# A new order table for an attention and feed-forward kernel: the step-2 load of w moves ahead of the first weights

## The chip, the cores and the metric

The kernel runs on 1 core of one Trainium2 chip. The metric is device time in microseconds (us) of one execution, the median of several runs. A core has five engines that run side by side and meet by semaphores: TensorE (PE, with its weight loads as PEld), VectorE (DVE), ScalarE (ACT), GpSimd (POOL) and SyncE (SP), which here issues all DMA transfers.

## The reference

Two stages, in float32. The first is a recurrent attention with 4 batches, 8 heads, 768 tokens and head size 48. The second is a feed-forward layer on the 3072 tokens with 384 features, whose weights go from 384 to 2048 and back.

```python
for t in range(S):                       # per batch b and head h
    y[t] = r[t] @ (state + outer(u * k[t], v[t]))
    state = w[t][:, None] * state + outer(k[t], v[t])
x = y as (3072, 384)
out = relu(x @ w_in) ** 2 @ w_out
```

## The kernel before

The tokens of a batch are cut into 3 steps of 256, so there are 12 steps, numbered 0 to 11; each works on all 8 heads. A step is a chain of some 40 short operations:

- **Loads** (`ld`, SP): w, r, k and v of a step come in four transfers of 384 KB each (line 212). u is one small row (line 240). The four groups of the first weights, `ld.0.i` to `ld.3.i` (line 220), and the four of the second, `ld.0.o` to `ld.3.o` (line 225), have 768 KB each. Each is cast to 16 bits by `cast` (line 232) on an engine that the order names.
- **Decay**: `ww_` multiplies neighbouring w (line 297), `lw_` takes the logarithm on ACT (301), `cum_` makes running sums by matmuls (341 to 345), `exp_` the exponential on ACT (358), `ni_` helps it on DVE in late steps (353), `ac_` the factors for the state (363). `rw_` and `kw_` are products of r and k with w (309, 313). `rd_` makes the decayed r and k on DVE (376).
- **Transposes of them**: steps 0 to 2 by matmuls (`tr_`, 385) and a copy (`rkt_`, 390). Steps 3 to 11 use two DMA transposes that SP issues (`dtr_`, 393).
- **Scores**: `p_` (410), then the mask product `pm_` on DVE (418 or 421).
- **Bonus term**: `ku_`, `qp_`, `q_`, `vq_` (316, 321, 324, 327).
- **State**: `su_` (433), `ts_` (441, 443), `sn_` (447).
- **Output of attention**: `y_`, `yq_`, `yc_`, `yb_`, `yd_` (460), copied by `ysb_` (510, 512). It is transposed by matmuls and a copy in steps 0 to 3 (`yt_` 520, `xt_` 525), by a DMA from step 4 on (`dyt_`, 528).
- **First layer**: `m1_`, 8 groups of 6 matmuls in a step, called expansion groups here (538). A group needs the cast weights of one of the four groups and one of four PSUM banks. `rl_` empties the bank with a relu (545 on ACT, 547 on DVE), `sq_` squares (553, 555).
- **Second layer**: steps 0 to 4 by `m2_`, 8 groups of 4 matmuls (561), emptied by `os_` (567, 569). Steps 5 to 11 use a scheme with 7 block products instead of 8: `tw_` and `sw_` make sums (580, 593), `pw_` are the products (615), `cx_` and `ow_` combine them (620 to 634).
- **Stores** (`store`, SP, 639), and **warm-up** matmuls without a result (`warm_`, 643).

No scheduler decides the order. It is written out as a string of 934 words, `ORDER`, and one loop turns each word into its instructions in turn. Each engine runs its own instructions strictly in that order, so an instruction that waits holds up all that stands behind it on its engine. A word can end with the engine (`=A` ACT, `=V` DVE, `=G` POOL) and can name its PSUM bank (`:2`).

```python
for word in ORDER.split():
    word, _, engine = word.partition("=")
    word, _, bank = word.partition(":")
    name, *args = word.split(".")
    args = tuple(int(x) if x.isdigit() else x for x in args)
    where[(name,) + args] = engine
    ...
    operations[name](*args)
```

So `rl_.5.3=A` is the relu of group 3 of step 5 on ScalarE. Buffers are handed out by a small helper in the same order: w, r, k and v have four buffers each, so that a load can run up to four steps ahead of its use.

Of the kernel before, what the change touches and what calls it, by code (L numbers as in the profile page):

```python
# [22 lines left out]
cast.i.0=A ld.2.r rkt_.1.1=V tr_.1.0:2 y_.0 rkt_.1.0=V yq_.0 ts_.0.1=V p_.1.1:n ku_.1=G ysb_.0.1=A p_.1.0:1 sn_.0.1=G
pm_.1.1 ysb_.0.0=A yt_.0.1:2 cast.i.2=A su_.1:0 yt_.0.0:3 xt_.0.1=V xt_.0.0=V qp_.1=V m1_.0.0:2 ts_.1.0=V cast.i.1=A
q_.1 sn_.1.0=G pm_.1.0 m1_.0.4:0 m1_.0.1:3 m1_.0.5:1 rl_.0.0=A m1_.0.2:2 vq_.1=G cast.i.3=A y_.1:1 rl_.0.1=V rl_.0.5=V
yc_.1 yq_.1 rl_.0.4=V yd_.1 ww_.2=V ld.0.o m1_.0.3:1 ld.2.v ysb_.1=A ts_.1.1=V m1_.0.7:3 ld.1.o lw_.2 rl_.0.3=V
sn_.1.1=G rl_.0.2=A yt_.1:0 kw_.2=G cum_.2:0 xt_.1=V m1_.0.6:1 rl_.0.7=V exp_.2 ld.4.w ld.3.w ld.2.o rd_.2.1 m1_.1.0:2
rw_.2=G rl_.0.6=A ld.3.o ku_.2=G rl_.1.0=A m1_.1.2:3 m1_.1.4:1 sq_.0.0=A rd_.2.0 tr_.2.1:0 m1_.1.6:2 rl_.1.2=V
rl_.1.4=A m1_.1.1:1 rl_.1.6=V qp_.2=G m1_.1.7:3 rkt_.2.1=V tr_.2.0:2 rl_.1.7=V v_.2=G m1_.1.3:0 rkt_.2.0=V cast.o.0=A
m1_.1.5:3 ac_.2 cast.o.1=G ld.3.k sq_.0.2=A sq_.0.1=A rl_.1.1=V m2_.0.1.0:2 rl_.1.3=A q_.2 sq_.1.0=A p_.2.1:0 su_.2:1  # L30
vq_.2=G sq_.1.1=A m2_.0.1.1 m2_.0.0.0:0 m2_.1.0.0:1 ts_.2.0=V ld.3.r sn_.2.0=G pm_.2.1 m2_.1.0.1 ww_.3=G yc_.2:1
sq_.0.3=A rl_.1.5=A cast.o.2=A yq_.2 p_.2.0:0 sq_.1.2=V m2_.0.0.1 m2_.1.1.0:3 pm_.2.0 lw_.3 sq_.1.3=A m2_.0.0.2
ww_.4=G cum_.3:0 ld.3.v ld.4.r ld.4.k exp_.3 kw_.3=G cast.o.3=A yb_.2 y_.2 m2_.1.1.1 ku_.3=V m2_.1.1.2 m2_.0.1.2
rd_.3.1 rw_.3=G ysb_.2=A lw_.4 m2_.0.1.3 m2_.1.1.3 dtr_.3.1 qp_.3=G rd_.3.0 cum_.4:1 ac_.3 exp_.4 os_.0.1=A os_.1.1=V
m2_.1.0.2 yt_.2:3 tw_.3=V m2_.0.0.3 xt_.2=A rw_.4=G q_.3 m2_.1.0.3 dtr_.3.0 os_.0.0=A kw_.4=G ku_.4=G m1_.2.2:3 ac_.4
os_.1.0=A rd_.4.0 m1_.2.0:0 rl_.2.2=A m1_.2.3:2 ld.4.v v_.3=A rd_.4.1 m1_.2.1:3 rl_.2.0=A su_.3:1 ld.5.w rl_.2.3=A
ld.5.k ld.5.r vq_.3=V p_.3.0:0 rl_.2.1=A ld.7.w m1_.2.6:1 m1_.2.4:2 ts_.3.0=V pm_.3.0 sq_.2.0=A sn_.3.0=G m1_.2.7:3
v_.4=G rl_.2.6=A ts_.3.1=V tw_.1=V yc_.3:1 yq_.3 sq_.2.1=A rl_.2.4=A rl_.2.7=A p_.3.1:0 m2_.2.1.0:0 m1_.2.5:1 ld.5.v
pm_.3.1 rl_.2.5=V ww_.5=G lw_.5 sq_.2.3=A qp_.4=V q_.4 sn_.3.1=G rw_.5=G kw_.5=G y_.3 store.0.1 yb_.3 su_.4:0 dtr_.4.0
m2_.2.0.0:2 ts_.4.0=V ww_.7=G ysb_.3=A m2_.2.0.1 sq_.2.2=A yt_.3:3 cum_.5:1 m2_.2.1.1 m2_.2.0.2 m2_.2.1.2 exp_.5  # L40
sn_.4.0=V store.1.1 rd_.5.1 dtr_.4.1 xt_.3=A m2_.2.1.3 ts_.4.1=V rd_.5.0 v_.5=G vq_.4=G ld.6.w os_.2.1=A m1_.3.4:1
m1_.3.2:3 m1_.3.0:0 ld.6.k rl_.3.4=A ac_.5 rl_.3.2=A rl_.3.0=A dtr_.5.1 sn_.4.1=V ku_.5=V qp_.5=V tw_.2=V m2_.2.0.3
su_.5:1 p_.4.1:0 m1_.3.5:3 ts_.5.0=V os_.2.0=A rl_.3.5=A m1_.3.1:0 pm_.4.1 m1_.3.3:2 dtr_.5.0 rl_.3.1=A m1_.3.7:3
sq_.3.0=A kw_.6=G rl_.3.3=V yc_.4:1 yq_.4 p_.4.0:0 m2_.3.1.0:1 pm_.4.0 sq_.3.2=A sq_.3.1=A rl_.3.7=A m1_.3.6:2 ld.6.r
ld.7.k ld.8.k ww_.6=G sn_.5.0=G ku_.6=G y_.4 yb_.4 ysb_.4=A q_.5 p_.5.0:0 pm_.5.0 store.2.1 m2_.3.1.1 m2_.3.0.0:0
vq_.5=G lw_.6 dyt_.4 tw_.4=V cum_.6:1 p_.5.1:0 rw_.6=G pm_.5.1 rl_.3.6=A exp_.6 m2_.3.0.1 m2_.3.0.2 m2_.3.1.2 ld.7.r
rd_.6.1 ku_.7=G lw_.7 sq_.3.3=A ld.6.v yc_.5:0 yq_.5 y_.5 m2_.3.1.3 dtr_.6.1 os_.3.1=A qp_.6=V rd_.6.0 kw_.7=G
# [653 lines left out]
```

## Time and profile before

| | |
|---|---|
| median of 3 runs | 178.3 us (177.92 to 178.44) |
| the profiled execution's own time | 178.94 us |
| its span, first to last instruction | 177.2 us |
| PE busy | 167.7 us (95%) |
| DVE busy | 148.6 us (84%) |
| ACT busy | 128.6 us (73%) |
| POOL busy | 113.1 us (64%) |
| DMA moved | 36.58 MB, mean 206 GB/s |
| granted TensorE clock, mean | 1.000 |

Busy time is the time in which an engine has an instruction under way. A row of the timeline reads: start in us from the span's start, duration in us, engine, line of the kernel, operation, out<-in, shapes, and in brackets the idle time of the engine just before it with what ended it. SPq is the queue in which SyncE issues transfers; its durations are those of the issue, not of the transfer. Matmuls are pipelined, so a row's duration for a group is a little longer than the distance to the next group.

### The profile page before, as it was taken

The page shows a single profiled execution, that of the slowest core. Times are in us where ns is not written, and L with a number is a line of the kernel's source. Part 1 is how long each engine was busy: PE and PEld are TensorE (multiplying, and loading weights), DVE is VectorE, ACT ScalarE, POOL GpSimd, SP SyncE. Part 2 cuts the span into 40 slices and gives each one's busy share as a digit, 9 for nine tenths or more (in the row PEclk, how much of TensorE's full clock was granted, in tenths as well). Part 3 has the DMA queues.
Part 4 walks back from the last instruction along what each step waited for, and adds up shares of the span by engine and source line. Part 5 has one row for each costly group of instructions (what it writes and reads, how often), then busy time and mean ns, then how long its engine had stood idle before and what let it go on. Part 6 is the DMA issues. An engine that isn't in the chain of part 4 may idle for free.

```text
span 177.2 us, 6475 instructions
## 1 busy us (share of the span) xinstructions
PE 167.7 (95%) x2772; PEld 132.9 (75%) x2774; DVE 148.6 (84%) x235; ACT 128.6 (73%) x213; POOL 113.1 (64%) x108
## 2 busy tenths in 40 slices
PE   7877899999999999999999999999999999999992
PEld 2344778756687686578866888878998988999991
DVE  5588998965999798989979998999989899559671
ACT  5574888989799579739697896888887584867200
POOL 6399359794974929997459367683547690572910
PEclk9999999999999999999999999999999999999999
DMA  5999999999998999998999999998697211420204
GB/s 151 315 311 350 367 266 357 230 369 286 218 257 233 237 256 191 304 253 101 286 199 306 233 156 286 172 238 236 134 257 67 51 45 41 140 89 4 89 10 167
DMA packets 82669, 36.58 MB, mean 206 GB/s; under 512 B 75857, under 2 KB 81106, under 8 KB 82642
## 3 DMA queue, kind: packets, MB, share of 16 engines
q1 hardware_dynamic: 82642, 36.19, 83.3%
q8 instruction: 21, 0.34, 0.8%
q14 instruction: 6, 0.05, 0.1%
HBM read 25.17 MB, written 4.72 MB: 169 GB/s over the span
## 4 chain that ended last, share of the span: by engine, by line
PE 76%; DMA 13%; POOL 4%; DVE 2%; SPq 1%; issue 1%; ACT 0%; DVEq 0%
PE one L538 29%; PE one L615 18%; PE one L561 15%; PE att L460 6%; DMA rkT_b<-rdec_buf 6%; DMA w_st_b<-in_moe_w_out_dram 5%; PE att L410 3%; DMA u_row<-in_u_dram 2%; PE att L433 2%; SPq L212 1%; POOL ku_b L316 1%; PE att L343 1%; POOL wo_sb L232 1%; DVE pmT_b L418 1%; POOL k_b L313 1%
## 5 line engine op out<-in xcount | busy, mean ns | idle before, releaser
L538 PE MATMUL one<-xT_b,wi_sb 128*128 128x256 bf16 x576 | 70.9, 273 | 0.5 <-DVE xT_b L525 0.5
L538 PEld LDWEIGHTS <-wi_sb 128*128 128x128 f16 x576 | 54.7, 98 | 9.1 <-issue 1.2
L545 ACT ACTIVATE gt_b<-one 128x512 f16<-128x512 f32 x73 | 42.1, 598 | 16.2 <-PE one L538 14.8
L553 ACT ACTIVATE gt_b<-gt_b 128x1024 bf16<-128x1024 f16 x39 | 40.1, 1052 | 0.1
L561 PE MATMUL one<-wo_sb,gt_b 128*128 128x384 f16 x160 | 29.5, 326 | 0.4 <-POOL wo_sb L232 0.4
L421 DVE TENSOR_TENSOR pmT_b<-att,mask 128x1024 bf16<-128x1024 f32 x22 | 26.8, 1218 | 1.9 <-PE att L410 1.8
L615 PEld LDWEIGHTS <-gt_b 128*128 128x128 bf16 x280 | 23.5, 98 | 0.6 <-issue 0.2
L561 PEld LDWEIGHTS <-gt_b 128*128 128x128 bf16 x160 | 14.8, 98 | 9.5 <-issue 0.6
L547 DVE TENSOR_SCALAR gt_b<-one 128x512 f16<-128x512 f32 x23 | 15.5, 684 | 3.2 <-ACT gt_b L545 1.9
L447 POOL TENSOR_TENSOR S_b<-t_b,ac_buf 128x192 bf16<-128x192 f32 x16 | 8.8, 551 | 13.8 <-DVE t_b L443 7.7
L327 POOL TENSOR_TENSOR vq_b<-v_b,q_b 128x768 bf16<-128x768 f32 x10 | 15.5, 1550 | 2.7 <-DVE q_b L324 2.7
L615 PE MATMUL one<-wo_sb,gt_b 128*128 128x192 f16 x168 | 16.5, 246 | 0.0
L316 POOL TENSOR_TENSOR ku_b<-k_b,u_bc 128x768 f32<-128x768 f32 x8 | 14.5, 1815 | 2.9 <-ACT u_bc L249 1.8
L313 POOL TENSOR_TENSOR k_b<-k_b,w_b 128x384 f32<-128x384 f32 x10 | 11.0, 1099 | 7.1 <-DMA k_b<-in_k_dram 7.1
L321 POOL TENSOR_TENSOR ku_b<-ku_b,r_b 128x768 f32<-128x768 f32 x8 | 14.9, 1858 | 0.5 <-DVE pmT_b L421 0.4
L309 POOL TENSOR_TENSOR r_b<-r_b,w_b 128x384 f32<-128x384 f32 x9 | 10.7, 1185 | 5.0 <-DMA r_b<-in_r_dram 4.8
L324 DVE TENSOR_REDUCE q_b<-ku_b 128x16 f32<-128x768 f32 x12 | 11.4, 946 | 1.7 <-POOL ku_b L321 1.7
L376 DVE TENSOR_TENSOR rdec_buf<-k_b,att 128x768 bf16<-128x768 f32 (+1 forms) x13 | 11.4, 885 | 1.0 <-POOL k_b L313 0.9
L376 DVE TENSOR_TENSOR rdec_buf<-r_b,att 128x768 bf16<-128x768 f32 (+1 forms) x13 | 11.5, 885 | 0.3 <-POOL r_b L309 0.3
L358 ACT ACTIVATE att<-att 128x768 f32<-128x768 f32 x12 | 9.6, 797 | 2.7 <-PE att L345 2.3
L615 PE MATMUL one<-w_st_b,gt_b 128*128 128x192 f16 x112 | 11.4, 246 | 0.0
L593 POOL TENSOR_TENSOR w_st_b<-w_st_b,gt_b 128x512 bf16<-128x512 bf16 x4 | 5.0, 1250 | 7.5 <-DVE w_st_b L593 7.5
(105 smaller groups left out, 281.8 us busy)
## 6 DMA issues: line engine op xcount, KB each, us to landing
w_b<-in_w_dram SPq DMA_DIRECT2D x12, 384.0 KB, 5.0
r_b<-in_r_dram SPq DMA_DIRECT2D x12, 384.0 KB, 5.0
k_b<-in_k_dram SPq DMA_DIRECT2D x12, 384.0 KB, 5.2
v_b<-in_v_dram SPq DMA_DIRECT2D x12, 384.0 KB, 4.5
out_dram<-w_st_b SPq DMA_DIRECT2D x23, 192.0 KB, 2.7
w_st_b<-in_moe_w_in_dram SPq DMA_DIRECT2D x4, 768.0 KB, 7.9
w_st_b<-in_moe_w_out_dram SPq DMA_DIRECT2D x4, 768.0 KB, 7.7
rkT_b<-rdec_buf SPq DMA_TRANSPOSE x18, 4.4
```

Of the source, the lines that this page charges most:

```text
L313: product("kw_", s)(k_raw[:, :, 0, :], k_raw[:, :, 1, :], w_raw[:, :, 1, :])
L316: product("ku_", s)(buf("ku", s)[:], buf("k", s)[:, :, 1:3, :], u_bc[:, :, None, :].to_broadcast([C, H, 2, D]))
L321: product("qp_", s)(ku[:], ku[:], buf("r", s)[:, :, 0:2, :])
L327: product("vq_", s)(buf("vq", s)[:].rearrange("p j h d -> p h j d"), buf("v", s)[:], buf("q", s)[:, :, :, None].to_broadcast([C, H, 2, D]))
L376: nc.vector.tensor_mul(rdec[:, i, :, heads, 0:D], x.rearrange("p h j d -> p j h d"), decay[:, None, :, :].to_broadcast([C, 2, n, D]))
L421: nc.vector.tensor_mul(pmT, ps_p[:].rearrange("p e (a x) -> p (e a) x", a=2), mk.to_broadcast([C, 4, 2 * C]))
L538: nc.tensor.matmul(ps1[:, j, :], wi_sb[:, n // 4, kk, n % 4 * 128:(n % 4 + 1) * 128], xT[:, :, kk, :], start=(kk == 0), stop=(kk == KT - 1))
L545: nc.scalar.activation(rl, m1, AF.Relu, scale=RS)
L547: nc.vector.tensor_scalar(out=rl, in0=m1, scalar1=RS, scalar2=0.0, op0=ALU.mult, op1=ALU.max)
L553: nc.scalar.activation(gt, rl, AF.Square)
L561: nc.tensor.matmul(m2, gt[:, n, c * C:(c + 1) * C], wo_sb[:, n, :], start=(n == 0), stop=(n == NT - 1))
L615: nc.tensor.matmul(where_to, gt[:, n, :], wo[:, n, :], start=(n == 0 and i in (1, 2, 5)), stop=(n == NT // 2 - 1), skip_group_check=True)
```

## The change

The string `ORDER` is replaced as a whole; all functions stay as they are. The new string has the same 934 words of work in another sequence, with other banks and, for some, another engine. Counted over the words: `qp_` 3 more on POOL and 3 fewer on DVE, `vq_` 2 more on POOL and 2 fewer on DVE, `rw_` 3 more on DVE and 3 fewer on POOL, `v_` 2 on DVE and 1 on ACT taken from POOL, `sq_` and `sw_` 3 each off DVE (to ACT and to POOL), `cast` 2 off ACT (one to POOL, one to DVE), `rl_` and `os_` 2 each from ACT to DVE. The warm-up matmuls are 28 instead of 24. One pair of lines of the diff stands for the rest:

```diff
-ld.0.w ld.0.r warm_.2.3 ld.0.k ld.0.u ww_.0=V lw_.0 ld.0.v warm_.9.0 rw_.0=G ld.1.w ld.1.r cum_.0:1 kw_.0=V exp_.0
+ld.0.w ld.0.k ww_.0=V warm_.7.2 ld.0.r warm_.3.1 ld.0.u ld.1.w lw_.0 ld.0.v cum_.0:0 ld.1.r exp_.0 warm_.4.2 rw_.0=V
```

First place: SyncE at the start of the program, the loads of steps 0 and 1 and the first of step 2. The buffers w_b_68, 69 and 70 hold w of steps 0, 1 and 2; the next transfers are the four groups of the first weights.

```order
 L212 DMA w_b_68<-in_w_dram 128x8x96
+L212 DMA k_b_76<-in_k_dram 128x8x96
 L212 DMA r_b_72<-in_r_dram 128x8x96
-L212 DMA k_b_76<-in_k_dram 128x8x96
 L240 DMA u_row<-in_u_dram 1x384
+L212 DMA w_b_69<-in_w_dram 128x8x96
 L212 DMA v_b_80<-in_v_dram 128x8x96
-L212 DMA w_b_69<-in_w_dram 128x8x96
 L212 DMA r_b_73<-in_r_dram 128x8x96
 L212 DMA k_b_77<-in_k_dram 128x8x96
+L212 DMA w_b_70<-in_w_dram 128x8x96
 L212 DMA v_b_81<-in_v_dram 128x8x96
```

k and r of step 0 change places (both stand ahead of u in either order), w of step 1 goes ahead of v of step 0, and w of step 2 is now ahead of v of step 1 and of the weights; before, it was issued behind all four weight groups.

Second place: ScalarE around the casts of the first weights (the w_st buffers), the y_sb copies of step 0 (y_sb_b_112, in two halves) and step 1 (y_sb_b_113), and the first evacuations (gt_b). First the rows of before:

```order
L305 CAST v_bf_b_91<-v_b_81 128x768
L232 CAST wi_sb<-w_st_b_84 128x1536
L512 CAST y_sb_b_112<-att_62 128x384 x2
L232 CAST wi_sb<-w_st_b_85 128x1536
L232 CAST wi_sb<-w_st_b_86 128x1536
L545 ACTIVATE gt_b_118<-one_66 128x512
L232 CAST wi_sb<-w_st_b_87 128x1536
L510 CAST y_sb_b_113<-att_63 128x768
```

And the rows of the changed kernel:

```order
L305 CAST v_bf_b_91<-v_b_81 128x768
L390 COPY rkT_b_101<-one_65 128x1024
L232 CAST wi_sb<-w_st_b_84 128x1536
L512 CAST y_sb_b_112<-att_62 128x384 x2
L232 CAST wi_sb<-w_st_b_85 128x1536
L232 CAST wi_sb<-w_st_b_86 128x1536
L232 CAST wi_sb<-w_st_b_87 128x1536
L545 ACTIVATE gt_b_118<-one_66 128x512
L301 ACTIVATE lw_buf_134<-ww_b_88 128x8x48
L510 CAST y_sb_b_113<-att_63 128x768
```

The evacuation that stood between the third and fourth cast moves behind the fourth, and the logarithm of step 2 goes ahead of the copy of step 1. The groups come in the order 0, 2, 1, 3 before and 1, 0, 2, 3 now; the expansion groups of step 0 are reordered to match (0, 4, 1, 5, 2, 3, 7, 6 before; 2, 0, 1, 5, 4, 7, 3, 6 now).

Third place: SyncE at the DMA transposes of steps 4 (rkT_b_100) and 5 (rkT_b_101), with stores of steps 0 to 2 (out_dram) and loads. First the rows of before:

```order
L639 DMA out_dram<-w_st_b_84 128x384
L393 DMA_TRANSPOSE rkT_b_100<-rdec_buf_140 128x8x128
L639 DMA out_dram<-w_st_b_84 128x384
L393 DMA_TRANSPOSE rkT_b_100<-rdec_buf_140 128x8x128
L212 DMA w_b_68<-in_w_dram 128x8x96
L212 DMA k_b_78<-in_k_dram 128x8x96
L393 DMA_TRANSPOSE rkT_b_101<-rdec_buf_141 128x8x128 x2
```

And the rows of the changed kernel:

```order
L639 DMA out_dram<-w_st_b_84 128x384
L393 DMA_TRANSPOSE rkT_b_100<-rdec_buf_140 128x8x128 x2
L393 DMA_TRANSPOSE rkT_b_101<-rdec_buf_141 128x8x128
L639 DMA out_dram<-w_st_b_84 128x384 x2
L393 DMA_TRANSPOSE rkT_b_101<-rdec_buf_141 128x8x128
L212 DMA w_b_71<-in_w_dram 128x8x96
```

The two transposes of step 5 stood next to each other behind two loads; now two stores stand between them. On TensorE the work between the running sums of step 5 and its first score matmuls becomes 3 output groups, 7 expansion groups and some small matmuls.

More of the change, by code (lines that the diff above doesn't have):

```diff
@@ L23 @@
[L23 to L47, printed above, removed]
@@ new lines @@
+yc_.0:0 tr_.1.1:0 yd_.0 yq_.0 rkt_.1.1=V y_.0 ts_.0.1=V p_.1.1:m sn_.0.1=G qp_.1=G cast.i.1=A pm_.1.1 ysb_.0.0=A
+ysb_.0.1=A p_.1.0:1 ld.3.w cast.i.0=A ld.2.v cast.i.2=A yt_.0.0:1 yt_.0.1:0 ww_.2=G su_.1:0 ld.2.r xt_.0.1=V xt_.0.0=V
+ts_.1.0=V q_.1 m1_.0.2:1 m1_.0.0:3 m1_.0.1:0 rl_.0.0=V pm_.1.0 vq_.1=G sn_.1.0=G m1_.0.5:2 ld.0.o m1_.0.4:3 rl_.0.1=V
+rl_.0.2=V cast.i.3=A ts_.1.1=V kw_.2=G rl_.0.5=A lw_.2 y_.1:1 yq_.1 yc_.1 ld.1.o yd_.1 m1_.0.7:2 ysb_.1=A ku_.2=V
+cum_.2:0 ld.3.r ld.3.k ww_.3=G rl_.0.7=A yt_.1:1 exp_.2 m1_.0.3:0 xt_.1=V m1_.0.6:2 rl_.0.3=A m1_.1.0:1 rd_.2.1
@@ L94 @@
+store.11.1.0
 """
```

119 lines of the change are left out of this document (69 added, 50 removed).

## The prediction, on record before the result

> **What bounds the kernel now.** I read the page first, then the busy time by stretch, then the timeline of the first 37 us and the chain that ended last. From the page: busy time of the engines, and two lines of the span in 40 slices of 4.43 us.
>
> ```profile
> PE 167.7 (95%) x2772; PEld 132.9 (75%) x2774; DVE 148.6 (84%) x235; ACT 128.6 (73%) x213; POOL 113.1 (64%) x108
> PE   7877899999999999999999999999999999999992
> DMA  5999999999998999998999999998697211420204
> ```
>
> TensorE is the bound: 167.7 of 177.2 us, with full slices from the fifth one on. The DMA line is full from the second slice to the twenty-eighth, so in the first 20 us transfers are what everything else runs after. The busy time by stretch (columns: stretch, length, then PE, PEld, DVE, ACT and POOL busy, clock, DMA share, GB/s) shows where TensorE still waits:
>
> ```profile
> 10.00:15.00 5.00, 3.38 (x66) 1.82 (x67) 4.62 (x7) 2.86 (x7) 5.00 (x6) 1.00 1.05 325
> 15.00:20.00 5.00, 3.98 (x147) 3.02 (x144) 4.11 (x9) 3.50 (x4) 3.84 (x4) 1.00 1.01 355
> ...
> 70.00:80.00 10.00, 9.87 (x174) 6.37 (x169) 8.52 (x10) 5.73 (x12) 9.64 (x8) 1.00 1.16 282
> ...
> 100.00:110.00 10.00, 9.60 (x196) 8.23 (x194) 9.35 (x15) 7.57 (x13) 5.26 (x5) 1.00 1.09 200
> 110.00:120.00 10.00, 9.59 (x231) 8.18 (x225) 9.11 (x15) 9.02 (x16) 7.76 (x8) 1.00 1.08 216
> ```
>
> From 40 to 170 us all other stretches are full, so the idle time there is 0.13 + 0.40 + 0.41 = 0.94 us. A matmul's modelled end overlaps the next one by about 0.2 us, so each wait is really that much longer than its idle time; five of them make about 2.0 us. That is all that a new order can win behind 40 us. Both orders hold the same TensorE work, but for four more warm-up matmuls. So the time is: the start of the dense stream, plus the same work, plus the waits in it. The timeline of before, around that start:
>
> ```profile
> 16.50 1.47 ACT L232 CAST wi_sb<-w_st_b 128x1536 f16<-128x1536 f32 x1 [2.37 <-DMA w_st_b<-in_moe_w_in_dram]
> ...
> 17.88 0.85 ACT L512 CAST y_sb_b<-att 128x384 bf16<-128x384 f32 x2
> ...
> 20.00 2.23 PE L538 MATMUL one<-xT_b,wi_sb 128*128 128x256 bf16 x19 [0.50 <-DVE xT_b L525]
> ...
> 20.77 1.47 ACT L232 CAST wi_sb<-w_st_b 128x1536 f16<-128x1536 f32 x1 [0.66 <-DMA w_st_b<-in_moe_w_in_dram]
> ```
>
> ScalarE idles 2.37 us for the first weight group, which lands at about 16.5; the third holds it up again, at 20.7. The first expansion matmul starts at 20.00, 1.27 us behind the end of the two y_sb copies (18.73).
>
> **The change, part by part.** *Loads.* A load of one step's input is 393 kB; at the 325 GB/s of the row 10 to 15 that is 1.21 us. The changed order puts w of step 2 ahead of the four weight groups, with the queues full (share 1.05), so I move every weight landing by +1.2: the first from 16.5 to 17.7, the third from 20.7 to 21.9. The bounds are 0 (a queue with room) and 1.3. The last cast of before shows no DMA wait and starts when the one ahead of it has long ended:
>
> ```profile
> 22.86 1.47 ACT L232 CAST wi_sb<-w_st_b 128x1536 f16<-128x1536 f32 x1
> ...
> 26.77 2.78 PE L538 MATMUL one<-xT_b,wi_sb 128*128 128x256 bf16 x24
> ```
>
> ScalarE idles from 22.74 to 22.86 there, so I take 22.8 as the landing of the fourth group, and 24.0 after the change. The swap of k and r of step 0 costs nothing: each is ahead of u before and after, and the two products change engines with them.
>
> *The chain to the first expansion matmul.* On ScalarE the cast of the first weights stands ahead of the y_sb copies of step 0, before as after. Before, it ended at 17.97 and the copies hardly waited. Now it runs from 17.7 to 19.2, the copies to 20.05, and with the same 1.27 us behind them the first expansion matmul starts at 21.3: **+1.3**. The cover for this delay is gone, since what stands ahead of it on TensorE is the same as before. The second mask of step 0 goes later as well; on VectorE five operations now stand between the two masks. The first fence has groups of the whole span (count, busy us, mean ns), the second rows of the timeline:
>
> ```profile
> L327 POOL TENSOR_TENSOR vq_b<-v_b,q_b 128x768 bf16<-128x768 f32 x10 | 15.5, 1550 | 2.7 <-DVE q_b L324 2.7
> L321 POOL TENSOR_TENSOR ku_b<-ku_b,r_b 128x768 f32<-128x768 f32 x8 | 14.9, 1858 | 0.5 <-DVE pmT_b L421 0.4
> ...
> L321 DVE TENSOR_TENSOR ku_b<-ku_b,r_b 128x768 f32<-128x768 f32 x4 | 4.4, 1096 | 0.0
> ...
> L309 DVE TENSOR_TENSOR r_b<-r_b,w_b 128x384 f32<-128x384 f32 x3 | 1.8, 590 | 0.0
> ```
> ```profile
> 10.04 1.22 DVE L421 TENSOR_TENSOR pmT_b<-att,mask 128x1024 bf16<-128x1024 f32 x1
> ...
> 12.81 0.95 DVE L324 TENSOR_REDUCE q_b<-ku_b 128x16 f32<-128x768 f32 x1 [0.36 <-POOL ku_b L321]
> ...
> 14.73 0.95 DVE L376 TENSOR_TENSOR rdec_buf<-r_b,att 128x768 bf16<-128x768 f32 x1
> ...
> 18.13 1.29 DVE L418 TENSOR_TENSOR pmT_b<-one,mask 128x512 bf16<-128x512 f32 x2 [0.24 <-PE one L410]
> ```
>
> From the first mask's end (11.26): 0.59 + 1.10 + 0.95 + 2 x 0.95 + 1.29 = 5.83, so 17.1 at the earliest (some waits between make it 17.5), and the step's output matmuls end at 18.0. That hides behind the cast, which ends at 19.2; it costs 0.6 only if the weights land as early as before. The four more warm-up matmuls (0.24 each, priced below) fall into the wait between the sums of step 1 at 12 and its transposes at 15: 0. The other changes of engine go together: 3 products at 1.86 and 2 at 1.55 come to POOL, smaller ones leave it, so it rises from 64% by some 3%, and DVE falls as much. None comes near TensorE's 95%, so they cost 0 in sum and act only through the waits below.
>
> *From there to 36 us.* All four casts now stand ahead of the first evacuation on ScalarE. The fourth runs from 24.0 to 25.5; behind it come an evacuation (0.59), a logarithm (0.53) and the y_sb copy of step 1 (0.80), to 27.4, and only then can its transposes run on TensorE, with the last two expansion groups of step 0 behind them in order. Transposes (0.35) and two groups (0.66 each) from 27.5 put the first group of step 1 at 29.1. Before, that group was the second in the row at 26.77, at 27.43: **+1.7**. Part comes back where before waited for the second output weights:
>
> ```profile
> 33.87 1.47 POOL L232 CAST wo_sb<-w_st_b 128x1536 f16<-128x1536 f32 x1 [1.23 <-DMA w_st_b<-in_moe_w_out_dram]
> ...
> 34.55 0.41 PE L433 MATMUL att<-v_bf_b,rdec_buf 64*64 64x48 bf16 x16
> ...
> 35.38 1.78 PE L561 MATMUL one<-wo_sb,gt_b 128*128 128x384 f16 x10 [0.42 <-POOL wo_sb L232]
> ```
>
> The 16 state matmuls issue in 0.19 us, so TensorE lost 0.65 there, of which I return 0.3 (o1 lands at nearly the same time, but its cast is now on ScalarE behind a square of 1.05). That leaves **+1.4** at 36 us.
>
> *Behind 36 us.* Three places have less cover and two more. (1) In step 2 exp of step 3 stands ahead of the y_sb copy, 0.80 each, and only two output groups (0.65 each) stand between the output matmuls and the transposes: 0.4, bounds 0 to 0.8. (2) The transposes by DMA of step 5:
>
> ```profile
> 58.52 0.32 PE L345 MATMUL att<-lw_buf,tri_incl_neg 128*128 128x384 bf16 x1
> ...
> 60.92 0.95 DVE L376 TENSOR_TENSOR rdec_buf<-r_b,att 128x768 bf16<-128x768 f32 x1
> ...
> 62.82 3.95 SPq L393 DMA_TRANSPOSE rkT_b<-rdec_buf  x2
> ...
> 70.30 0.42 PE L410 MATMUL att<-rkT_b 64*64 64x128 bf16 x16
> ```
> ```profile
> 65.52 4.74 DMA rkT_b<-rdec_buf
> ```
>
> Before, 11.5 us pass from the end of the sums (58.84) to the score matmuls (70.30), and they wait about 0.2. After, TensorE holds 8.8 us of work there: 7 expansion groups x 0.66, 3 output groups x 0.65, and 2.2 of small matmuls. The chain needs exp (0.80), two decays (0.95 each), the first transpose's issue (1.3), two stores (1.1 each), then 4.74 with the last transpose: 10.9 at worst; with the stores issued early, 8.7. I take a wait of 0.8 instead of 0.2, so +0.6 (0 to 1.9). (3) At step 11 the copy (0.8) and the transpose stand against 7 groups of 0.66 = 4.6; before, 10 groups covered it.
>
> ```profile
> xT_b<-y_sb_b SPq DMA_TRANSPOSE x8, 3.8
> ```
>
> 0.8 + 3.8 + 0.2 makes +0.2 (0 to 0.7). In return, the idle 0.81 of the rows 100 to 120 can go. One of its two waits is this one, in the chain and the timeline:
>
> ```profile
> 109.79 5.81 DMA rkT_b<-rdec_buf
> ```
> ```profile
> 115.65 0.64 PE L410 MATMUL att<-rkT_b 64*64 64x128 bf16 x32 [0.41 <-DMA rkT_b<-rdec_buf]
> ```
>
> Step 9 had 10.5 us of TensorE work over its transposes and has 12.5 now. The other is an evacuation queued on VectorE behind other work, which a new order shuffles. I take -0.8 (0 to -0.94, or to -2.0 with the overlaps). The last 18 product groups and the stores behind them end in the same words, so the tail gets 0.
>
> **Sum:** 1.4 + 0.4 + 0.6 + 0.2 - 0.8 = +1.8 on the span of 177.2, so 179.0. The profiled execution took 178.94, 1.74 more than its span; the runs' median, 178.3, is 0.64 under it. I add the difference to the median: **180.1 us**.
>
> **The rivals.** *Faster: the later waits go.* If steps 5 to 11 of the new order find transposes and evacuations always in time, 2.0 us vanish, none of the three new waits comes, and 178.3 + 1.4 - 2.0 = 177.7. It decides at an idle sum under 0.1 us from 40 to 170. For it: steps 3, 6 and 9 have 2 to 3.5 us more cover. Against: steps 5, 8, 10 and 11 have 1 to 5 us less. Chance 0.20. *No change: the weights come no later.* Should the queue absorb w of step 2, the first expansion matmul is late by only the 0.6 of the mask. The wait of 0.65 at 35 us then absorbs that, and the later terms stay at +0.4: 178.3 + 0.6 - 0.65 + 0.4 = 178.6. Against it stands the share of 1.05. It also stands for the case that the moved load does nothing. Chance 0.17. *Much slower: a new wait in mid-stream.* If the step 5 transposes take their worst, +1.9, and one more place like it loses 0.6, the time is 178.3 + 1.4 + 0.4 + 1.9 + 0.6 - 0.4 = 182.2, with half of the 0.8 won back. Chance 0.15. *Slower: a cold clock.* The warm-up matmuls show two speeds:
>
> ```profile
> 1.19 4.24 PE L643 MATMUL one<-warm 128*128 128x512 bf16 x11 [1.19 <-DVE warm L267]
> ...
> 12.28 1.89 PE L643 MATMUL one<-warm 128*128 128x512 bf16 x8
> ```
>
> They come at 0.39 us each at first and 0.24 later. Between 18.4 and 21.3 TensorE has about 1.2 us of work after the change, and if the clock fell there, five groups would cost 0.66 more each, partly hidden by the weights: +1.7, so 181.8. Every stretch above has a granted clock of 1.00, with waits up to 0.7 us. Chance 0.06. The Trainium skill, "TensorE: Matmul & The Clock Gate", part 1 on the HAM clock gate, says the clock halves after an idle window of about 3.4 us and needs as long a busy one to return. By it the gap of 2.9 us, broken by short transposes, is just too short; the trace agrees on the first 4 us of half speed, and shows no fall.
>
> **How the numbers follow.** The forecast has the rest, 0.42, and its own range is 179.2 to 181.3. Faster by over 0.3% (0.53 us, about what a measurement of this kernel can tell from no change) is 0.20, within it 0.17, slower 0.42 + 0.15 + 0.06 = 0.63. For 8 in 10 the range takes in the faster rival's middle and most of the slow one: 177.6 to 182.4.
>
> **What would show it.** Right: the first weight cast starts near 17.7 with a DMA wait, the first expansion matmul near 21.3, the first of step 1 near 29.1, and TensorE idles more in 15 to 30 than before. Score matmuls of step 5 wait for a transpose; those of step 9 don't. Wrong in the first step: a first matmul at 20.0 to 20.5. Wrong in the later ones: idle time from 40 to 170 far from 0.94 + 0.4.

## The result, and the profile after

The changed kernel takes 181.98 us (median of 4 runs, 181.6 to 182.97); the kernel before took 178.11 in the runs beside it. The ratio is 1.0249, with a 95% interval from 1.0212 to 1.0287: slower by 3.9 us in the medians (4.4 by the ratio), where +1.8 was forecast. Below, a time is the median over all runs of a kernel; a ratio to the kernel before, with its 95% interval, leaves out runs over 1.5% above the fastest of their kernel, and a difference said to be by the ratios comes from two of them.

The profiled execution of after took 182.97 us with a span of 181.0, against 178.94 and 177.2 of before. From its page, the busy time of the engines and two lines of the span in 40 slices, now 4.53 us each:

```profile
PE 171.3 (95%) x2778; PEld 134.5 (74%) x2778; DVE 141.2 (78%) x231; ACT 130.4 (72%) x215; POOL 119.4 (66%) x110
PE   7998699999999999999989989999996999999993
PEclk9999669999999999999999999999999999999999
```

Two things were not there before: a clock of 6 in the fifth and sixth slices, and a 6 in TensorE's line at the 31st, near 138 us. The busy time by stretch (columns as in the prediction):

```profile
15.00:20.00 5.00, 2.83 (x105) 2.15 (x103) 3.64 (x7) 3.55 (x5) 4.69 (x5) 0.93 1.01 351
20.00:25.00 5.00, 4.84 (x56) 3.47 (x54) 2.75 (x6) 2.95 (x3) 2.59 (x3) 0.50 1.04 338
25.00:30.00 5.00, 5.00 (x120) 3.96 (x119) 3.43 (x6) 3.99 (x6) 2.63 (x2) 0.89 0.88 238
...
90.00:100.00 10.00, 9.29 (x124) 6.81 (x121) 8.66 (x14) 9.05 (x16) 6.73 (x5) 1.00 1.11 242
100.00:110.00 10.00, 9.54 (x192) 7.97 (x191) 6.94 (x14) 8.23 (x14) 5.05 (x6) 1.00 0.83 172
...
130.00:140.00 10.00, 8.83 (x137) 8.10 (x135) 6.58 (x13) 7.96 (x14) 6.29 (x6) 1.00 0.88 167
```

From 20 to 25 us TensorE looks busy, 4.84 of 5, but at half the clock: a busy share says nothing of speed. Behind 40 us the idle time stands at 90 to 110 and 130 to 140. The timeline of after around the start:

```profile
17.84 1.47 ACT L232 CAST wi_sb<-w_st_b 128x1536 f16<-128x1536 f32 x1 [1.45 <-DMA w_st_b<-in_moe_w_in_dram]
...
19.21 0.85 ACT L512 CAST y_sb_b<-att 128x384 bf16<-128x384 f32 x2
...
19.74 0.88 PE L520 MATMUL one<-ident,y_sb_b 128*128 128x128 bf16 x6 [1.92 <-ACT y_sb_b L512]
...
21.33 5.73 PE L538 MATMUL one<-xT_b,wi_sb 128*128 128x256 bf16 x30 [0.16 <-DVE xT_b L525]
...
22.02 1.47 ACT L232 CAST wi_sb<-w_st_b 128x1536 f16<-128x1536 f32 x1 [0.54 <-DMA w_st_b<-in_moe_w_in_dram]
...
25.18 1.47 ACT L232 CAST wi_sb<-w_st_b 128x1536 f16<-128x1536 f32 x1 [1.69 <-DMA w_st_b<-in_moe_w_in_dram]
```

The first cast waits until 17.8, the two y_sb copies stand behind it, and the first expansion matmul comes at 21.33. But TensorE has idled 1.92 us ahead of its transposes, and 30 matmuls (five groups) take 5.73 us, against 3.75 in `e1_warm` below, where the clock stays at 1.00.

Behind 60 us, the waits of TensorE (us in total, times, longest):

```profile
PE att L460 <- DVE pmT_b L421: 1.4, 1, 1.4
PE att L341 <- DVE t_b L443: 0.7, 1, 0.7
PE att L410 <- DMA rkT_b<-rdec_buf: 0.5, 1, 0.5
```

These are one wait each, of steps 10, 8 and 8 again, and none is at a place that the prediction priced. The first and the last lead back to a DMA, as the chain that ended last says (start, length, what); what stands ahead of the other on VectorE is shown with its experiment.

```profile
103.21 4.31 DMA rkT_b<-rdec_buf
...
134.20 4.42 DMA out_dram<-w_st_b
```

The longest in the timeline, step 10:

```profile
134.20 0.57 SPq L639 DMA_DIRECT2D out_dram<-w_st_b  x1
...
138.71 0.36 DVE L634 SCALAR_TENSOR_TENSOR w_st_b<-one,w_st_b 128x192 f32<-128x192 f32 x1 [2.67 <-DMA out_dram<-w_st_b]
...
138.98 1.21 DVE L421 TENSOR_TENSOR pmT_b<-att,mask 128x1024 bf16<-128x1024 f32 x1
...
140.25 0.31 PE L460 MATMUL att<-S_b,rkT_b 64*64 64x48 bf16 x16 [1.42 <-DVE pmT_b L421]
```

The first half of the store of step 2 is issued at 134.20 and lands at 138.62; in before the same store is issued at 77.51. VectorE's output sum of step 7 needs that buffer and waits 2.67 us at the head of its queue, with the mask of step 10 behind it, for which TensorE waits. A store that nobody waits for has become the critical path through a buffer and an in-order queue.

### The profile page after: what moved, and what is told of

The parts are those of the page before. It is cut to its first block, busy times and chain, and to the rows that moved or that the text cites. A ratio compares the mean times of both kernels' runs of the same rounds, so it can differ in the third digit from the quotient of the medians.

```text
span 181.0 us, 6497 instructions
## 1 busy us (share of the span) xinstructions
PE 171.3 (95%) x2778; PEld 134.5 (74%) x2778; DVE 141.2 (78%) x231; ACT 130.4 (72%) x215; POOL 119.4 (66%) x110
## 4 chain that ended last, share of the span: by engine, by line
PE 76%; DMA 9%; SPq 6%; DVE 5%; issue 2%; ACT 0%; DVEq 0%
PE one L538 32%; PE one L615 17%; PE one L561 14%; PE att L460 6%; SPq L212 5%; DMA w_st_b<-in_moe_w_in_dram 4%; PE att L410 3%; DMA out_dram<-w_st_b 2%; DMA rkT_b<-rdec_buf 2%; DVE pmT_b L421 2%; PE att L433 1%; PE one L520 1%; PE att L343 1%; SPq L240 1%; PE att L345 1%
## 5 line engine op out<-in xcount | busy, mean ns | idle before, releaser
L538 PE MATMUL one<-xT_b,wi_sb 128*128 128x256 bf16 x576 | 72.9, 279 | 0.2 <-DVE xT_b L525 0.2
L538 PEld LDWEIGHTS <-wi_sb 128*128 128x128 f16 x576 | 55.8, 100 | 9.6 <-issue 0.3
L553 ACT ACTIVATE gt_b<-gt_b 128x1024 bf16<-128x1024 f16 x42 | 43.6, 1054 | 1.1 <-DVE gt_b L547 1.0
L561 PE MATMUL one<-wo_sb,gt_b 128*128 128x384 f16 x160 | 29.5, 327 | 0.0
L321 POOL TENSOR_TENSOR ku_b<-ku_b,r_b 128x768 f32<-128x768 f32 x11 | 20.9, 1901 | 3.2 <-DVE ku_b L316 3.2
L447 POOL TENSOR_TENSOR S_b<-t_b,ac_buf 128x192 bf16<-128x192 f32 x16 | 10.3, 644 | 17.9 <-DVE t_b L443 14.7
L561 PEld LDWEIGHTS <-gt_b 128*128 128x128 bf16 x160 | 14.8, 98 | 8.6
L327 POOL TENSOR_TENSOR vq_b<-v_b,q_b 128x768 bf16<-128x768 f32 x12 | 18.4, 1535 | 3.7 <-DVE q_b L324 2.6
L547 DVE TENSOR_SCALAR gt_b<-one 128x512 f16<-128x512 f32 x25 | 16.8, 683 | 3.1 <-PE one L538 2.9
L316 POOL TENSOR_TENSOR ku_b<-k_b,u_bc 128x768 f32<-128x768 f32 x7 | 12.7, 1821 | 0.0
L297 POOL TENSOR_TENSOR ww_b<-w_b 128x384 f32<-128x384 f32 x8 | 8.7, 1081 | 2.4 <-DMA w_b<-in_w_dram 2.4
L620 ACT ACTIVATE w_st_b<-one 128x192 f32<-128x192 f32 x11 | 3.6, 328 | 9.1 <-PE one L615 5.3
```

The costliest lines, as they stand in the source:

```text
L316: product("ku_", s)(buf("ku", s)[:], buf("k", s)[:, :, 1:3, :], u_bc[:, :, None, :].to_broadcast([C, H, 2, D]))
L321: product("qp_", s)(ku[:], ku[:], buf("r", s)[:, :, 0:2, :])
L327: product("vq_", s)(buf("vq", s)[:].rearrange("p j h d -> p h j d"), buf("v", s)[:], buf("q", s)[:, :, :, None].to_broadcast([C, H, 2, D]))
L538: nc.tensor.matmul(ps1[:, j, :], wi_sb[:, n // 4, kk, n % 4 * 128:(n % 4 + 1) * 128], xT[:, :, kk, :], start=(kk == 0), stop=(kk == KT - 1))
L547: nc.vector.tensor_scalar(out=rl, in0=m1, scalar1=RS, scalar2=0.0, op0=ALU.mult, op1=ALU.max)
L553: nc.scalar.activation(gt, rl, AF.Square)
```

## The experiments

The edits are to the order table; the words are as there (`ld` load, `cast.i` cast of expansion weights, `ysb_` copy, `ts_`/`sn_` state, `dtr_` transposes by DMA, `warm_.n.b` n warm-up matmuls into bank b; where an expectation says the store of a group, it is that of a step). The theory: a start that is late (weights, copies behind a cast, half clock) and later waits that the new places of stores and loads make. The rival: all of it is the start, and the clock most of all.

**1. Keep the clock up in the gap** (`e1_warm`).

```diff
-ysb_.0.1=A p_.1.0:1 ld.3.w
+ysb_.0.1=A p_.1.0:1 warm_.8.1 ld.3.w
```

> The changed kernel with 8 warm-up matmuls more, placed on TensorE between the last score matmuls of step 1 (17.8 us) and the y_sb transposes of step 0 (19.7 us), where it idles 1.9 us. Both theories expect the granted clock to stay at 1.00 and the first five expansion groups to take 0.66 us each instead of 1.25. Clock theory (the half-speed clock is the cost): the 2.3 us of the profile come back, in the runs' median about 1.6, so 180.4. Weights theory (the late weights bind TensorE with or without the clock): TensorE then waits for the casts of the weights, the first group of step 1 moves only from 30.9 to 30.1, so 181.2, gain 0.3 to 0.8.

Measured: 181.91, ratio 1.0243 [1.0186, 1.0300]. Its stretch from 20 to 25 us, and two rows of its timeline:

```profile
20.00:25.00 5.00, 4.51 (x89) 3.60 (x91) 4.23 (x8) 3.86 (x3) 2.53 (x4) 1.00 1.01 314
```
```profile
27.35 4.09 PE L538 MATMUL one<-xT_b,wi_sb 128*128 128x256 bf16 x36
...
35.09 0.81 PE L561 MATMUL one<-wo_sb,gt_b 128*128 128x384 f16 x4
```

The clock stays at 1.00. The row of 36 holds two groups of step 0 and four of step 1, so the first of step 1 starts 1.31 behind its start: 28.66. And the median does not move: the other three runs of after had a mean clock of 0.991, by estimate some 3.3 us at half speed, against 0.981 and 6.8 us in the profiled one, and spans of 179.7 to 180.3, little above the 179.6 here. So the clock is not what makes the loss of 3.9 us, and that rival falls; what a short stretch at half speed costs is below what these runs can tell.

**2. The load of w of step 2 back behind the weights** (`e2_w2_back`), **and the same with the product that reads it moved as well** (`f2_start`).

```diff
-ub_:0 ld.1.k ld.2.w uc_=A
+ub_:0 ld.1.k uc_=A
-ld.3.i exp_.1 ld.2.k
+ld.3.i ld.2.w exp_.1 ld.2.k
```
and, in `f2_start` alone,
```diff
-ww_.2=G su_.1:0
+su_.1:0
-vq_.1=G sn_.1.0=G
+vq_.1=G sn_.1.0=G ww_.2=G
```

> The changed kernel with one word moved: the load of w of step 2 goes back behind the four first weight groups. Weights theory: the first cast starts at 16.6 instead of 17.8, the first expansion matmul at 20.2 instead of 21.3, TensorE idles under 1 us before it so that the clock stays at 1.00, and the first group of step 1 starts near 28.0 instead of 30.9; 2 to 3 us come back, so 179.0 to 180.0. If the early load was not the cause of the lag: 181.5 or more.

> After with w of step 2 behind the four first-weight loads, as in before, and with the product that reads it on GpSimd moved behind v*q and the last state sum of step 1, so that nothing is queued behind it early. Theory (the load ahead of the weights costs the start): first expansion matmul at 19.3 to 19.6, clock at 1.00 throughout, no wait of 2.4 us at the bonus matmuls of step 1, the first group of step 1 at 27.5 to 28.7, 179.8 to 180.8. Rival (the order on ScalarE and TensorE sets the start, not the load): first group of step 1 still at 29.5 or later, 181.4 to 182.2.

Measured: `e2_w2_back` 183.81, ratio 1.0346 [1.0288, 1.0404]; `f2_start` 181.82, ratio 1.0214 [1.0159, 1.0269]. The timeline of `e2_w2_back`:

```profile
23.88 0.99 POOL L297 TENSOR_TENSOR ww_b<-w_b 128x384 f32<-128x384 f32 x1 [4.31 <-DMA w_b<-in_w_dram]
...
24.83 1.47 POOL L327 TENSOR_TENSOR vq_b<-v_b,q_b 128x768 bf16<-128x768 f32 x1
...
26.36 0.36 PE L460 MATMUL att<-vq_b,ident 64*64 64x384 bf16 x4 [2.30 <-POOL vq_b L327]
```

GpSimd stands 4.31 us before a product that needs w, with v*q behind it: the changed order needs the early load. With the product moved, this wait goes, and step 2 is late instead:

```profile
23.55 1.47 ACT L232 CAST wi_sb<-w_st_b 128x1536 f16<-128x1536 f32 x1 [1.00 <-DMA w_st_b<-in_moe_w_in_dram]
...
31.57 0.95 DVE L376 TENSOR_TENSOR rdec_buf<-r_b,att 128x768 bf16<-128x768 f32 x1 [1.31 <-POOL r_b L309]
```

The first group of step 1 starts at 28.52, nearly as with the load early and the clock up (28.66 in `e1_warm`). Moving the load back does not buy the start back: one load's place is not a term that stands alone.

**3. That load early in the kernel before** (`e3_before_w2_early`).

```diff
-ld.3.i ld.2.w cum_.1:0
+ld.3.i cum_.1:0
-ub_:0 ld.1.k rd_.0.0.1
+ub_:0 ld.1.k ld.2.w rd_.0.0.1
```

> The kernel before with the same one word moved the other way: w of step 2 ahead of the last load of step 1 and of the first weights. Weights theory: the first cast starts at 17.7 instead of 16.5, the first expansion matmul at 21.3 instead of 20.0, and 1.2 to 3 us are lost, 179.3 to 181; the clock falls only if TensorE idles close to 2 us before it. If the rest of the new order makes the lag: 178.1 as before.

Measured: 178.71, ratio 1.0034 [0.9991, 1.0077]. First and last weight cast:

```profile
17.08 1.47 ACT L232 CAST wi_sb<-w_st_b 128x1536 f16<-128x1536 f32 x1 [2.11 <-DMA w_st_b<-in_moe_w_in_dram]
...
24.12 1.47 ACT L232 CAST wi_sb<-w_st_b 128x1536 f16<-128x1536 f32 x1 [1.17 <-DMA w_st_b<-in_moe_w_in_dram]
```

Against 16.50 and 22.86 of before that is +0.6 and +1.3, the price forecast for a load, and the first group of step 1 comes at 27.86 instead of 27.43. The wait for the output weights at 35 us is gone from the trace, so it can have absorbed the rest.

**4. The later waits, repaired** (`e4_store_early`: the store of step 2 alone; `f1_late`: that store, the state of step 7 ahead of the reduction q of step 7, and the store of step 4 behind the second transpose of step 8).

```diff
-dtr_.11.1 store.2.0 ow_.6.2
+dtr_.11.1 ow_.6.2
-store.1.0 ld.8.k
+store.1.0 store.2.0 ld.8.k
```
and, in `f1_late`, also
```diff
-dtr_.7.1 q_.7 ts_.7.1=V
+dtr_.7.1 ts_.7.1=V q_.7
-p_.7.1:0 store.4.1 m1_.6.5:0 pm_.7.1 dtr_.8.1
+p_.7.1:0 m1_.6.5:0 pm_.7.1 dtr_.8.1 store.4.1
```

> The changed kernel with one store moved: that of the second half of step 2 goes from behind the transposes of step 11 to behind the first store of step 1, some 48 us earlier. Theory: the wait of 1.6 us on TensorE at 138.7 to 140.2 comes from this store, whose buffer the first result of step 7 needs; with it gone 1.2 to 1.6 us come back, so 180.5. Rival (the mask product of step 10 is late for its own reasons, or the next wait takes its place): 181.7 or more.

> After with three later edits, the start untouched: the second half store of group 2 right behind the first of group 1; the rescaling of the state of step 7 on VectorE ahead of the reduction q of step 7; the store of group 4 behind the second transpose of step 8. Theory (the later waits cost 3 us, about 2 more than those of before): the waits at the sums of step 8, the scores of step 8 and the correction product of step 10 go, 179.4 to 180.6. Rival (each wait that goes is made good by another, as when one store was moved earlier): 181.4 to 182.2 with new waits named in the trace.

Measured: `e4_store_early` 182.21, ratio 1.0276 [1.0214, 1.0338]; `f1_late` 181.07, ratio 1.0141 [1.0071, 1.0212]. The store alone left the time where it was, as its rival said. In both the wait of step 10 is gone, and in `f1_late` that at the scores of step 8; in both a new one came at a transpose of step 9, 0.2 in `e4_store_early` and 0.6 in `f1_late`. The wait at the sums of step 8 stayed. First VectorE in after, ahead of the sums at 94.32, then the same place in `f1_late`:

```profile
91.72 0.95 DVE L316 TENSOR_TENSOR ku_b<-k_b,u_bc 128x768 f32<-128x768 f32 x1
...
93.06 0.94 DVE L324 TENSOR_REDUCE q_b<-ku_b 128x16 f32<-128x768 f32 x1
93.92 0.34 DVE L443 TENSOR_TENSOR t_b<-S_b,att 128x192 f32<-128x192 bf16 x1
```
```profile
91.80 0.96 DVE L316 TENSOR_TENSOR ku_b<-k_b,u_bc 128x768 f32<-128x768 f32 x1 [0.92 <-DMA k_b<-in_k_dram]
...
93.14 0.35 DVE L443 TENSOR_TENSOR t_b<-S_b,att 128x192 f32<-128x192 bf16 x1
```

The state operation, which reads the bank that the sums then take, went ahead of the reduction, and the product in front of both then waited 0.92 for k of step 8, landed at 91.78. The edit was right about the queue and did not help while that load was late: it is word 433 of the new order, and 355 of the old.

**5. The copies of step 0 ahead of the first cast** (`h1_copies_first`), **and that with the three later edits** (`h2_late_copies`).

```diff
-cast.i.1=A pm_.1.1 ysb_.0.0=A ysb_.0.1=A p_.1.0:1
+pm_.1.1 ysb_.0.0=A ysb_.0.1=A cast.i.1=A p_.1.0:1
```

> After with one edit: on ScalarE the first weight cast stands behind the two y_sb copies of step 0 instead of ahead of them. Theory (copies queued behind a cast that waits for late weights leave TensorE idle for 1.9 us, and the clock falls): copies at 17.6 to 18.6, transposes at 18.8, the first expansion matmul at 20.1 to 20.6, clock 1.00 in all stretches, first group of step 1 at 28.0 to 28.8, and 179.7 to 180.8. Rival (the weights and casts behind it bind anyway): the first expansion matmul as said, but the first group of step 1 still at 28.7 or later and 181.4 to 182.2.

> The same edit together with the three later ones (store of group 2 early, state of step 7 ahead of the reduction q, store of group 4 behind the transpose of step 8). If the two add up, 177.6 to 179.0: 2.0 less than the copies-first kernel, with the clock at 1.00. If the later gain of the first trial (0.9 in the median, more in its runs of full clock) was chance, 180.0 to 181.2.

Measured: `h1_copies_first` 182.34, ratio 1.0239 [1.0183, 1.0294]; `h2_late_copies` 179.18, ratio 1.0093 [1.0055, 1.0131]. In both the long gap is gone and the first expansion matmul comes at 19.5, 1.8 earlier than in after, yet the first group of step 1 only at 28.4 and 28.3: the fourth cast (23.6) and the copy of step 1 behind it hold it there. That is where the theory had this group, yet `h1_copies_first` is no faster than after, as its rival said; why the earlier start brings nothing is open. The later edits on top of it take off 2.6 us by the ratios. In the profile of `h2_late_copies` no wait of TensorE behind 60 us is left, and the stretches that had them are full:

```profile
90.00:95.00 5.00, 4.91 (x57) 3.38 (x59) 4.81 (x8) 4.97 (x10) 4.76 (x4) 1.00 1.27 210
95.00:100.00 5.00, 5.00 (x84) 3.59 (x77) 3.77 (x5) 4.29 (x7) 2.65 (x3) 1.00 1.02 226
100.00:110.00 10.00, 10.00 (x202) 8.70 (x201) 8.21 (x15) 9.07 (x17) 7.80 (x8) 1.00 0.89 221
...
130.00:140.00 10.00, 10.00 (x230) 8.75 (x229) 8.34 (x14) 8.18 (x15) 7.49 (x7) 1.00 0.60 95
```

**6. Halves of one order with halves of the other** (`g1_before_then_after`, `g2_after_then_before`, `h4_before_start`; `h5_start_late` is the latter with the later edits). Their edit is too long for a diff: the words of one kernel up to a named one, then the words not yet done in the other's order. In `g1_before_then_after` the bonus product of step 3 overwrites the bank with one half of that step's scores before its mask has read them; the instructions are all there.

> The order of before up to the first score matmuls of step 3 (some 50 us), and from there on all that is left in the order of after. If the loss is shared by the start and by the later waits (cum of step 8, scores of step 8, the correction product of step 10), this comes out about half way, 179.6 to 180.6. If the whole loss is made in the first 37 us, it equals before, 177.8 to 178.6. If it is made by the later waits alone, it equals after, 181.5 to 182.2. The three later waits should be there as in after, 0.8 + 0.7 + 1.4 us.

> The other half: the order of after up to the product v*q of step 3 (some 53 us), then what is left in the order of before. Shared loss: 179.6 to 180.6, and the two differences to before add up to after's +3.9. All of it in the start: 181.5 to 182.2. Nothing of it in the start: 177.8 to 178.6. The waits at the sums of step 8, the scores of step 8 and the correction product of step 10 should be gone.

> The order of before up to the first state tile of step 2 (some 32 us), then what is left in the order of after. No wait is expected at the seam, unlike at the seam near 50 us. By the shares read from the traces (start 2.0 to 2.5 of the 3.9, later waits 1.5 to 1.9) 179.4 to 180.4. If the start costs nothing in the end: 181.4 to 182.2. If it is all: 177.8 to 178.6.

> The same, with the three later edits as well. If start and later waits are the whole loss, this equals before: 177.4 to 178.6, possibly below it, with no wait of over 0.7 us behind 50 us. If 179 or more is left, something in the changed order outside these places costs time.

Measured: 181.81, ratio 1.0222 [1.0167, 1.0277]; 183.02, 1.0306 [1.0248, 1.0365]; 186.68, 1.0511 [1.0473, 1.0549]; 183.97, 1.0346 [1.0307, 1.0385]. All four made waits of their own at the seam, up to about 3 us, so they do not divide the loss. `h4_before_start` shows how:

```profile
34.68 1.00 POOL L297 TENSOR_TENSOR ww_b<-w_b 128x384 f32<-128x384 f32 x1 [2.96 <-DMA w_b<-in_w_dram]
35.62 0.82 POOL L305 CAST v_bf_b<-v_b 128x768 bf16<-128x768 f32 x1
...
36.50 0.62 PE L433 MATMUL att<-v_bf_b,rdec_buf 64*64 64x48 bf16 x16 [2.77 <-POOL v_bf_b L305]
```

Again a product that waits for a load, with a cast behind it that TensorE needs. Of use is the pair: with the same seam, the three later edits took 2.9 us off by the ratios.

**7. The short gaps filled** (`k1_copies_fill`, `k2_late_copies_fill`, on top of the two kernels of 5; `h3_late_warm`: `f1_late` with the filler of 1; `k3_before_no_fill`: before with a filler less).

```diff
-su_.1:0
+su_.1:0 warm_.3.2
-m1_.0.2:1
+m1_.0.2:1 warm_.2.2
```
and, in `k3_before_no_fill`,
```diff
-pm_.0.0 warm_.9.3 ac_.1
+pm_.0.0 ac_.1
```

> After with the copies of step 0 ahead of the first cast, and three and two warm-up matmuls in the gaps behind the state products of step 1 and behind the first expansion group. Theory (the clock falls in some executions of the copies-first order, and that alone keeps its median up): clock 1.00 in all runs, 180.3 to 181.2, 1.2 to 2.0 below the copies-first kernel. Rival (its slower runs have another cause, such as late transfers): median again 181.8 to 182.8, with the clock at 1.00.

> The same with the three later edits. Theory: clock 1.00 in all runs, 177.6 to 178.7, equal to the kernel before within the interval; the changed order then has no loss left but these edits. Rival: 179.0 to 180.0 as without the fillers.

> After with the three later edits and eight warm-up matmuls in the gap ahead of the y_sb transposes of step 0; the copies stay behind the cast. Against the kernel with the eight warm-up matmuls alone (181.9), the later edits at a steady clock: theory 179.2 to 180.0 (2.0 to 2.7 less); rival (a median that other waits hold up) 181.0 to 182.0.

> Before without the nine warm-up matmuls ahead of the transposes of step 1, so that TensorE is idle from about 12.1 to 14.7 us, 2.6 us. If such a gap lowers the clock here too: 0.50 in the stretch from 15 to 19 us, the first expansion matmul 0.5 to 1.5 later than 20.0, and 178.6 to 180.0. If only longer gaps do, clock 1.00 and 177.3 to 178.2.

Measured: `k1_copies_fill` 182.01, ratio 1.0263 [1.0217, 1.0309]; `k2_late_copies_fill` 180.08, 1.0150 [1.0114, 1.0185]; `h3_late_warm` 181.83, 1.0202 [1.0144, 1.0260]. By the ratios none came down against the same kernel without the filler, although the mean clock was 0.996 or more in every run of the first two: the clock is not what holds them up. `k3_before_no_fill`: 179.98, ratio 1.0129 [1.0083, 1.0176]. Its clock in 40 slices, and the end of its gap:

```profile
PEclk9995579999999999999999999999999999999999
```
```profile
14.40 1.03 PE L385 MATMUL one<-ident,rdec_buf 128*128 128x128 bf16 x8 [2.56 <-DVE rdec_buf L376]
```

Idle for 2.56 us, then half clock for about 10 us: 2.3 us dearer by the ratio. The warm-up matmuls in before are worth that.

**8. The transposes of step 7 issued early** (`l1_late_copies_tr7` on `h2_late_copies`, `l2_copies_tr7` on `h1_copies_first`). In the profile of `h3_late_warm`, the scores of step 7 had waited for them; it is one execution, of 184.03 us where the median is 181.83:

```profile
PE att L410 <- DMA rkT_b<-rdec_buf: 2.3, 1, 2.3
```

```diff
-ld.8.r
+ld.8.r dtr_.7.0 dtr_.7.1
-su_.7:1 dtr_.7.0
+su_.7:1
-sq_.5.3=A dtr_.7.1
+sq_.5.3=A
```

> After with the copies of step 0 ahead of the first cast, the three later edits, and the two transposes of step 7 issued right behind the load of r of step 8, ahead of the other loads and stores there. Theory (late issue of these transposes is the wait that differs from run to run): issues at 85 to 88 us, no wait at the scores of step 7, 177.4 to 178.6, 0.6 to 1.8 below the same kernel without it, and no run over 179.5. Rival (the spread comes from the loads at the start): 179.0 to 179.8 with the same spread.

> The same edit without the three later ones. Theory: the runs at a clock of 0.99 go, and the median comes from 182.3 to the full-clock runs of the copies-first kernel, 180.4 to 181.2, with the waits at the sums of step 8, the scores of step 8 and the correction product of step 10 still there. Rival: 181.8 to 182.8.

Measured: 183.33, ratio 1.0283 [1.0241, 1.0326], and 185.09, ratio 1.0411 [1.0365, 1.0457]: by the ratios 3.4 and 3.1 us slower than without, on another chip. The waits from 88 to 97 us in `l1_late_copies_tr7`:

```profile
ACT w_st_b L567 <- DMA out_dram<-w_st_b: 3.2, 1, 3.2
...
PE one L538 <- ACT w_st_b L567: 2.0, 1, 2.0
```

The transposes went ahead of the stores of steps 1 and 2 on SyncE's queue, the first of these stores landed at 91.75 (87.11 without the edit), and ScalarE's output copy waited for the buffer with the evacuations behind it. The theory that these transposes make the spread fell; the spread of the runs within a kernel (179.22 to 183.27 in `f1_late`) stays open.

## Why the prediction was wrong

The measured time lies inside the stated range of 177.6 to 182.4, but the loss is about twice the forecast, and it was not made where the forecast put it. The traces can be cut at one event, the first output-product group of step 0 (L561, 4 matmuls; 35.09 in the row of `e1_warm`). In before it is:

```profile
33.56 0.81 PE L561 MATMUL one<-wo_sb,gt_b 128*128 128x384 f16 x4
```

The same row in the other profiles, and what is left of the span behind it:

| profile | at, us | span behind it, us |
|---|---|---|
| before | 33.56 | 143.6 |
| before, w early (`e3`) | 33.99 | 141.9 |
| before, filler less (`k3`) | 36.07 | 141.6 |
| after | 37.09 | 143.9 |
| after, gap filled (`e1`) | 35.09 | 144.5 |
| after, load back (`f2`) | 35.99 | 143.8 |
| store early (`e4`) | 37.08 | 142.8 |
| copies first (`h1`) | 34.56 | 143.9 |
| copies first, filled (`k1`) | 35.20 | 145.2 |
| late edits (`f1`) | 36.16 | 142.6 |
| copies first, late edits (`h2`) | 34.57 | 141.2 |
| the same, filled (`k2`) | 34.78 | 142.3 |

TensorE has done nearly the same work by then: 96 expansion matmuls in before and 90 in after, one group of 0.66 less, against 32 short score and state matmuls more. Each row is one execution. Not in the table are the orders with a seam or with the moved transposes, `e2_w2_back`, and `h3_late_warm`, which has the late edits and yet 146.4: that execution waited 2.3 at the transposes of step 7, and its clock fell after it.

Behind the event the changed order without late edits takes 143.8 to 145.2, mean 144.3, the old order 141.6 to 143.6, mean 142.4, and the changed order with all three late edits 141.2 to 142.6, mean 142.0: in these executions the late waits are worth about 2 us, and with them repaired the new order is level with the old behind the event.

- **Weights land 1.2 later.** Right: 17.84 for the first cast against 17.7 forecast, 22.02 for the third against 21.9; the fourth at 25.18, forecast 24.0, was at 23.9 in `e1_warm`. The DMA brought 84 GB/s from 25 to 26 us in after; why is open.
- **First expansion matmul at 21.3.** Right: 21.33, by the chain told (cast, copies, 1.27 us).
- **First group of step 1 at 29.1, +1.4 at 36 us.** Right in the mechanism, and in size where the clock held: 28.66 and +1.5 at the event in `e1_warm`. In the profiled execution it was 30.92 and +3.5. The difference is the half clock and not the late fourth group: `e4_store_early` has the same fall of the clock, its fourth cast at 24.06, and the event at 37.08. This was the cold-clock rival, with a chance of 0.06 that was too small. It needed no gap of 2.9 us; 1.92 was enough. Yet it does not make the loss: with the gap filled the ratio is 1.0243.
- **Behind 36 us: +1.2 for three places, -0.8 in return, net +0.4.** This step failed. TensorE shows no wait at step 2, at the transposes of step 5 or at step 11. Instead 0.79 came at the sums of step 8, 0.62 at its scores and 1.59 at the correction product of step 10 (starts against the work ahead of them), 3.0 in sum. What the prediction put at nothing, without a reason, is the order inside the queues of SyncE and VectorE: it counted only the cover over transposes, not what waits behind an operation that itself waits for a buffer or a load. The first half of the store of step 2 went from word 404 to word 710, the load of k of step 8 from 355 to 433. The prediction does say that the transposes of step 8 lose cover, but gives them no price. Its sentence that the changes of engine "cost 0 in sum" is not refuted by this: the output sum, the product and the state operation that wait are on VectorE in both orders.
- **The -0.8 in return.** Wrong in another way. Half of it was a transpose wait of 0.41 in the profile of before, which neither `e3` nor `k3` shows at its later part, both made of the same order there. A gain that exists in one execution was subtracted from the median of all. The other half, a wait of 0.4 for an output sum on VectorE, stands in both and is gone in after.
- **The rivals.** By their number two are equally near to 181.98: the new wait in mid-stream (182.2) and the cold clock (181.8). The clock did fall, but filling its gap changed the time by less than can be told, so that agreement is luck. The new waits came, at other places and by another way than the one priced.
- **What makes up the 3.9 us.** Some 1.5 are the start and about 2 the late waits. By the ratios the three late edits together took off 2.6 (`h1` to `h2`), 2.9 (`h4` to `h5`), 2.0 (`k1` to `k2`) and 2.3 (`l2` to `l1`), each pair on one chip. Outside such pairs they took off 1.9 and 0.7 (after to `f1`, `e1` to `h3`), so their size without the copies edit stays uncertain, and no run tells the three waits apart. That the start costs 1.5 is read from traces. In the old order a late start reached the end: in `k3` the event comes 2.5 later, and the time is 2.3 longer. In the new order the event came 1.1 to 2.5 earlier with the gap filled, the load moved with its product, or the copies moved, and the ratios stayed within 0.0035 of after's, 0.6 us. So the share of the start is not shown by a run, and the rest of the loss is not placed.

No version beat the kernel before; the nearest, `h2_late_copies`, is 0.9% slower.

## What to carry to other kernels

When an order of work changes, list for every operation that waits for a buffer or a load what stands behind it in its engine's queue: a late store becomes critical through the buffer that it frees, and moving one transfer ahead on a shared queue makes another late. Before subtracting a wait from a forecast, ask whether a second execution would show it. And read the granted clock beside the busy share of every gap.

## What the runs showed of the hardware

TensorE's granted clock fell to 0.50 around idle times of 1.66 us (`f1_late`, idle until 19.6, clock down from 21.6), 1.92 us (after), 2.30 us (`e2_w2_back`, at 25 us), 2.56 us (`k3_before_no_fill`) and 2.77 us (`h4_before_start`). It stayed there for 3.4 us in `f1_late` and `e2_w2_back`, 6.8 us in after and `h4_before_start`, and 10.2 us in `k3_before_no_fill`, which are one, two and three times 3.41 us. Idle times of 1.42 us (after, near 139), 1.67 us (`g1_before_then_after`, at 54 us), 2.04 us (`l1_late_copies_tr7`, at 91 us) and 2.23 us (`l2_copies_tr7`, at 91 us) left it at 1.00, so the length of the gap alone does not decide; what else does, no run here shows. The prediction had taken from the Trainium skill, "TensorE: Matmul & The Clock Gate", part 1, that the clock halves after an idle window of about 3.4 us. Here 1.66 us was enough once, and the measurement decides. A half clock of 10.2 us made before 2.3 us longer; in after, filling the gap changed the ratio only from 1.0249 to 1.0243.

The same loads, in the same order, landed at different times in two executions: k of step 1 at 11.38 in `e2_w2_back` and at 12.53 in `f2_start`, whose orders are alike up to there. SyncE had already issued it 0.82 us apart, at 6.53 and 7.35.
